# Routing sums its logits by matrix products and takes row numbers from the one-hot; one k load and one transposing transfer are ordered behind the first expert's weights

## The chip, the cores and the metric

The kernel runs on one core of a Trainium2 chip. Times are device microseconds of that core, from the start to the end of one launch. Engines are named as in the profile: PE multiplies matrices (PEld is its loading of the stationary operand), DVE, ACT and POOL do elementwise work, and SP issues most of the DMA transfers in this kernel (some are issued from ACT's queue). Each engine and each queue takes its instructions in a fixed order.

## The reference

Three layers follow one another. The first is attention with random features, for 4 batches of 8 heads, 576 rows and 64 columns: `phi(x) = exp(x·omega − |x|²/2 − max)`, then `kv = phi(k)ᵀ·v`, `num = phi(q)·kv`, divided by `phi(q)·Σphi(k)`. The second is a mixture of 8 experts over the 2304 resulting rows of 512 columns:

```python
logits = x @ w_gate
expert_idx = np.argmax(logits, axis=1)
probs = softmax(logits); gate_w = probs[row, expert_idx]
out[mask] = gate_w[mask, None] * (np.maximum(xe @ w1[e], 0.0) @ w2[e])
```

The third is a dense layer `(h * sigmoid(1.702 h)) @ w_out` with `h = x @ w_in` and 2048 columns in the middle.

## The kernel before

Attention is done in eight steps, two for each batch, of four heads each. `kgen(i)` does the k side of step i (projections "P" in `ph_P`, then `kv`), `qgen(i)` the q side (projections P, transposes X, the product N with `kv`, and the transposes R of the finished rows into `xh` and `xl`). Inputs are loaded by `load_qk` (L237). From the sixth operand on, `halves_T` (L286) splits an operand into two halves of 16 bits (ACT L297, POOL L298) and turns them by a transposing DMA issued on SP (L299); the turned tile `xT` has three buffers, so a transfer waits until the projections of three operands ago are through.

When a batch of 576 rows is done, `route_steps(b)` (L510) finds its expert. The logits come as two parts, from the high and the low half of `w_gate`, in one tile `lT` of 16 rows (8 experts by two parts) and 576 columns. Five PE transposes (L527) turn `lT`, DVE copies the result (L532, L533) and adds the two parts (L535). A row maximum (L539) and a comparison (L541) give the one-hot `oh`. A product with ones (L551) counts the rows of each expert, DVE finds the most frequent expert and writes its number `es` (L558 to L561), SP loads that number into a register (L594), and `pump` and `stage` (L669, L650) then issue the loads of this expert's weights (L664). For the rows that chose otherwise (`eq`, `rr`, a general path at the end), the number of each row's own expert is needed: five times a maximum of eight and an index search on DVE (L578, L579), and a copy (L581).

The expert's weights come in 8 parts (4 of `w1`, 4 of `w2`). For the first batch the first part is loaded in two pieces; the first seven parts have places of their own, so that eight transfers can be issued at once. Each part is split into high (ACT L686) and low (L688, on DVE for the first part and for the last batch's expert, else on POOL), and `moe_gen` multiplies (L128, tile `m_ps`, three products for each operand pair).

The program is written as generators: `attention_gen` merges `qgen(i)`, `kgen(i+1)` and a pending `route` by weight, and from the end of the first routing on a planner takes turns between attention and experts by the work done on each side. A scheduler then fixes the order on each engine by its own timeline; `tc.high_priority()` lifts the loads of the first expert's weights (L661). A manual dependency of the kind `NoSync` between two instructions only fixes their order in that schedule.

Of the kernel before, what the change touches and what calls it, by code (L numbers as in the profile page):

```python
# [8 lines left out]
F32 = mybir.dt.float32  # L9
# [13 lines left out]
def kernel(  # L23
# [91 lines left out]
    def behind(ins, n):  # L115
# [3 lines left out]
        for x in found:  # L119
# [3 lines left out]
                reason="behind",  # L123
            )

    def mm3(ps, ah, al, bh, bl, start, stop, pin=False):
# [45 lines left out]

    QH = 4
    NJ = 9
    NQ = B * (H // QH)
    clock = [0]
    late = []

# [55 lines left out]

    NB = QH * T + 2

    def load_qk(src, dst, i):  # L237
        b, qd = divmod(i, H // QH)
        h0 = qd * QH
        m = att.tile([P, NB, D], F32, tag="m", name="m", bufs=2)  # L240
        step = 2 if i < 1 else QH
        for h in range(0, QH, step):
            nc.sync.dma_start(
                out=m[:, h * T:(h + step) * T].rearrange("p (h t) d -> p h (t d)", h=step),
                in_=src[b, h0 + h:h0 + h + step, 0:T * P, :].rearrange("h (p t) d -> p h (t d)", t=T),
            )
        for pr in range(2):
            nc.sync.dma_start(
                out=m[pr * TAIL:(pr + 1) * TAIL, QH * T:],
                in_=src[b, h0 + 2 * pr:h0 + 2 * pr + 2, T * P:S, :].rearrange("h s d -> s h d"),  # L250
            )
        dst[i] = m

    sides = [0]
# [28 lines left out]
            square_sum(m, c, sq, FOLD)  # L283
        src[i] = (xT, sq, True)

    def halves_T(src, i, eng):  # L286
        sides[0] += 1
        if sides[0] <= FPX:
            return turned(src, i)
        if sides[0] - 1 in LO_DVE:  # L290
            eng = nc.vector
        m = src[i]
        hl = att.tile([P, NB, 2, D], F16, tag="hl", name="hl", bufs=2)
        xT = att.tile([P, NB, P], F16, tag="xT", name="xT", bufs=3)
        sq = att.tile([P, NB], F32, tag="sq", name="sq", bufs=3)
        for c in (slice(0, 8), slice(8, NB)) if i < FINE else (slice(0, NB),):
            nc.scalar.activation(out=hl[:, c, 0], in_=m[:, c], func=ACTF.Copy)  # L297
            eng.tensor_tensor(out=hl[:, c, 1], in0=m[:, c], in1=hl[:, c, 0], op=ALU.subtract)  # L298
            XQ.dma_start_transpose(out=xT[:, c], in_=hl[:, c].rearrange("p n a d -> p (n a d)"))  # L299
            square_sum(m, c, sq, FOLD_LATE)  # L300
        src[i] = (xT, sq, False)

# [101 lines left out]
    def qgen(i):  # L404
        b, qd = divmod(i, H // QH)
        qi = i
        if i + 1 < NQ:
            load_qk(q, q_in, i + 1)
            halves_T(q_in, i + 1, nc.vector if i + 1 < DVE_LO else nc.gpsimd)
# [60 lines left out]
        for n, op in enumerate(Q_ORDER.split()):  # L470
            g = int(op[1])
            if op == "R0" and qd == 0:
                while x_done[0] < b - 1:
                    yield None
                xh_t[b] = (moe if b % 2 else xep).tile([P, KD, S], F32R, tag="xh", name="xh", bufs=1)
                xl_t[b] = (moe if b % 2 else xep).tile([P, KD, S], F32R, tag="xl", name="xl", bufs=1)
            if op[0] == "P":
                c = ph_P(i, src, qp, "qp", 3, g)
            else:
                c = {"X": X, "N": N, "R": XT}[op[0]](g)  # L480
            if n == 0 and i + 1 < NQ:
                load_v(i + 1)
            if n == KPRE and i + 2 < NQ:
                load_qk(k, k_in, i + 2)
                halves_T(k_in, i + 2, nc.vector if i + 2 < DVE_LO else nc.gpsimd)
            yield c
        c0 = qd * QH * D
# [9 lines left out]


    gate_t, reg_t = {}, {}

    def route(b):
        g = route_steps(b)
# [7 lines left out]
    def route_steps(b):  # L510
# [10 lines left out]
            nc.scalar.activation(out=lT[:, c], in_=lT_ps, func=ACTF.Copy)  # L521
        yield 2.0
        yield 0
        lg_ps = pp.tile([P, T + 1, 2, E], F32, tag="n", name="lg_ps", bufs=1)
        for t in range(T + 1):
            n = P if t < T else TAIL
            nc.tensor.transpose(  # L527
                lg_ps[:n, t].rearrange("p a e -> p (a e)"), lT[:, t * P:t * P + n], ident[:2 * E, :2 * E]
            )
        lg2 = att.tile([P, T + 1, 2, E], F32, tag="lg2", name="lg2", bufs=1)  # L530
        nc.vector.memset(lg2[:, T], 0.0)
        nc.vector.tensor_copy(lg2[:, 0:T], lg_ps[:, 0:T])  # L532
        nc.vector.tensor_copy(lg2[:TAIL, T], lg_ps[:TAIL, T])  # L533
        lg = att.tile([P, T + 1, E], F32, tag="lg", name="lg", bufs=1)
        nc.vector.tensor_tensor(out=lg, in0=lg2[:, :, 0], in1=lg2[:, :, 1], op=ALU.add)  # L535


        rm = att.tile([P, T + 1, 1], F32, tag="rm", name="rm", bufs=2)
        nc.vector.tensor_reduce(out=rm, in_=lg, axis=AX.X, op=ALU.max)  # L539
# [35 lines left out]
        mx = att.tile([P, T + 1, 8], F32, tag="lmx", name="lmx", bufs=1)  # L575
        ix = att.tile([P, T + 1, 8], U32, tag="lix", name="lix", bufs=1)
# [73 lines left out]
    def stage(b, c):  # L650
        e = reg_t[b]
        if c < NW:
            st = landing(b, c, [P, KD, nfw * P])
            src = w1[bass.ds(e, 1), :, c * nfw * P:(c + 1) * nfw * P].rearrange("o (k p) f -> p (o k) f", p=P)
        else:
            c2 = c - NW
            st = landing(b, c, [P, nfw, DM])
            src = w2[bass.ds(e, 1), c2 * nfw * P:(c2 + 1) * nfw * P, :].rearrange(
                "o (k p) d -> p (o k) d", p=P
            )  # L660
        with tc.high_priority() if b in HP_STAGE else nullcontext():  # L661
# [326 lines left out]
    if True:  # L988
# [6 lines left out]
        halves_T(q_in, 0, nc.vector if DVE_LO else nc.gpsimd)  # L995
        load_qk(k, k_in, 1)
        setup_wg()
        halves_T(k_in, 1, nc.vector if DVE_LO else nc.gpsimd)
        A, Mg = attention_gen(), moe_all()
        done_a = done_m = 0.0  # L1000
# [532 lines left out]
```

## Time and profile before

| | before |
|---|---|
| median of 3 runs | 769.03 us (768.45 to 770.22) |
| the profiled execution's own time | 769.27 us |
| its span, first to last instruction | 767.3 us |
| PE busy | 740.3 us (96%) |
| PEld busy | 717.7 us (94%) |
| DVE, ACT, POOL busy | 529.7 (69%), 338.2 (44%), 131.9 us (17%) |
| share of PE in the chain that ended last | 84% |
| mean granted clock of PE | 0.989 of full speed |

How to read it: the time outside the span is 1.97 us in this execution. PE is at work nearly all the time, so what a change is worth shows in the few stretches where PE stands still or has the lower clock, and in the number and length of PE's own instructions.

### The profile page before, as it was taken

How to read it: one execution, taken by the hardware profiler on the slowest of the kernel's cores; microseconds unless marked ns; L12 is line 12 of the kernel's file. 1: busy time of each engine (PE TensorE's matmuls, PEld its weight loads, DVE VectorE, ACT ScalarE, POOL GpSimd, SP SyncE). 2: the span in 40 equal slices, each digit the busy share in tenths (PEclk: the TensorE clock that was granted, in tenths of full speed). 3: DMA queues.
4: the chain of work that ended last, by engine and by line, in shares of the span. 5: the costliest groups of instructions: out<-in, count | busy, mean ns of one | idle time of the engine just before them, and what ended most of it. 6: DMA issues, size and time to landing. Idle time of an engine off the chain costs nothing.

```text
span 767.3 us, 14364 instructions
## 1 busy us (share of the span) xinstructions
PE 740.3 (96%) x5559; PEld 717.7 (94%) x5559; DVE 529.7 (69%) x1188; ACT 338.2 (44%) x638; POOL 131.9 (17%) x78
## 2 busy tenths in 40 slices
PE   7998699999999999999999999999999999999997
PEld 6877599999999999998999999999999999999997
DVE  5877767485876686565879649981368777777774
ACT  5555354334621432233427464454576434443331
POOL 3564277608600441000000000000000000000000
PEclk9999789999999999999999999999999999999999
DMA  6447683447825454199245558972978544443311
GB/s 157 119 132 183 160 264 84 133 118 218 184 60 161 142 186 126 49 247 283 60 152 187 186 179 277 326 256 100 343 263 302 176 138 138 136 123 122 116 29 32
DMA packets 136716, 127.59 MB, mean 166 GB/s; under 512 B 58176, under 2 KB 120896, under 8 KB 135744
## 3 DMA queue, kind: packets, MB, share of 16 engines
q1 hardware_dynamic: 123936, 98.85, 43.8%
q10 hardware_dynamic: 12704, 27.73, 10.3%
q8 instruction: 46, 0.75, 0.4%
q14 instruction: 30, 0.25, 0.1%
HBM read 79.68 MB, written 40.40 MB: 156 GB/s over the span
## 4 chain that ended last, share of the span: by engine, by line
PE 84%; DVE 7%; DMA 5%; ACT 1%; issue 1%; POOL 0%; SPq 0%; ACTq 0%; POOLq 0%
PE m_ps L128 19%; PE qa L1237 13%; PE qa L1134 13%; PE qm L1237 7%; PE w_ps L128 4%; PE pb L1237 3%; PE qm L1134 3%; PE num L434 3%; PE qu L1134 3%; PE kv_ps L392 3%; DMA st<-in_moe_w_dram 2%; PE pr L334 2%; PE qn L1134 2%; PE tq L420 2%; PE qt L1134 2%
## 5 line engine op out<-in xcount | busy, mean ns | idle before, releaser
L1134 PE MATMUL qa<-y,wi 128*128 128x384 f32 x576 | 109.2, 337 | 0.4 <-DVE g L889 0.4
L1134 PEld LDWEIGHTS qa<-y,wi 128*128 128x128 f32 x576 | 101.4, 188 | 0.8 <-DVE g L889 0.8
L128 PE MATMUL m_ps<-xh,wh 128*128 128x288 f32 x256 | 80.3, 314 | 6.6 <-ACT wh L686 4.2
L128 PE MATMUL m_ps<-xh,wl 128*128 128x288 f32 x256 | 77.9, 304 | 0.0
L128 PE MATMUL m_ps<-xl,wh 128*128 128x288 f32 x256 | 77.2, 302 | 0.0
L688 POOL TENSOR_TENSOR wl<-st,wh 128x1024 fp32r<-128x1024 f32 x23 | 55.2, 2405 | 85.9 <-ACT wh L686 84.5
L349 DVE TENSOR_REDUCE small<-pr 128x4 f32<-128x512 f32 (+1 forms) x80 | 51.1, 638 | 9.6 <-PE pr L341 6.0
L128 PEld LDWEIGHTS m_ps<-xh,wh 128*128 128x128 f32 x256 | 49.5, 193 | 8.3 <-ACT wh L686 4.4
L686 ACT ACTIVATE wh<-st 128x1024 fp32r<-128x1024 f32 (+1 forms) x33 | 33.8, 1032 | 49.4 <-DMA st<-in_moe_w_dram 33.7
L723 DVE SCALAR_TENSOR_TENSOR h1l<-m_ps,h1h 128x288 fp32r<-128x288 f32 x64 | 28.8, 453 | 30.3 <-ACT h1h L720 30.3
L128 PEld LDWEIGHTS m_ps<-xl,wh 128*128 128x128 f32 x256 | 49.4, 193 | 0.2
L128 PEld LDWEIGHTS m_ps<-xh,wl 128*128 128x128 f32 x256 | 49.4, 193 | 0.2
L720 ACT ACTIVATE h1h<-m_ps 128x288 fp32r<-128x288 f32 x64 | 25.7, 407 | 51.8 <-PE m_ps L128 49.9
L128 PE MATMUL m_ps<-h1h,wh 128*128 128x288 f32 x160 | 48.3, 302 | 0.0
L128 PE MATMUL m_ps<-h1l,wh 128*128 128x288 f32 x160 | 48.1, 301 | 0.0
L128 PE MATMUL m_ps<-h1h,wl 128*128 128x288 f32 x160 | 47.8, 299 | 0.0
L1237 PE MATMUL qa<-p,p 128*128 128x256 f32 x360 | 46.1, 283 | 1.1 <-DVE p L843 0.8
L1237 PE MATMUL qa<-p,gs 128*128 128x256 f32 x360 | 45.9, 282 | 0.0
L1237 PEld LDWEIGHTS qa<-p,p 128*128 128x128 f32 x360 | 44.2, 190 | 1.6 <-DVE p L843 1.0
L1237 PEld LDWEIGHTS qa<-p,gs 128*128 128x128 f32 x360 | 44.2, 189 | 0.0
L434 PEld LDWEIGHTS num<-kv,qpT 128*128 128x128 f32 (+1 forms) x320 | 37.1, 186 | 5.4 <-ACT qpT L422 2.7
L434 PE MATMUL num<-kv,qpT 128*128 128x65 f32 (+1 forms) x320 | 39.5, 268 | 2.3 <-ACT qpT L422 1.4
(213 smaller groups left out, 1817.3 us busy)
## 6 DMA issues: line engine op xcount, KB each, us to landing
g_dram<-g ACTq DMA_DIRECT2D x48, 384.0 KB, 4.1
st<-in_moe_w_dram SPq DMA_DIRECT2D x31, 512.0 KB, 4.9
pg<-g_dram SPq DMA_DIRECT2D x10, 1024.0 KB, 5.5
raw<-in_moe_w_in_dram SPq DMA_DIRECT2D x16, 512.0 KB, 4.1
gt<-g_dram SPq DMA_DIRECT2D x8, 1024.0 KB, 5.5
p<-wo_dram SPq DMA_DIRECT2D x6, 1024.0 KB, 7.2
yt<-y_dram SPq DMA_DIRECT2D x12, 384.0 KB, 6.0
vm<-in_v_dram SPq DMA_DIRECT2D x32, 128.0 KB, 3.1
```

The lines of the kernel that those rows point to most:

```text
L128: ins = nc.tensor.matmul(out=ps, lhsT=a, rhs=b, start=start and n == 0, stop=stop and n == 2)
L334: nc.tensor.matmul(out=ps[:, :, h2], lhsT=xT[:, (2 * pr + h2) * 2 + t0 // 2], rhs=wbd)
L349: nc.vector.tensor_reduce(out=pm, in_=ps[:, :w], axis=AX.X, op=ALU.max, negate=on_act)
L392: nc.tensor.matmul(out=kv_ps[:, h, :], lhsT=kp[j // 2][:, j % 2, h2, :], rhs=vm[:, h, t, :], start=(t == 0), stop=False,)
L420: nc.tensor.transpose(tq[:, c, h2], qp[i][:, c, h2, :], ident)
L434: nc.tensor.matmul(out=ps[:n, c, h2, :], lhsT=lhsT, rhs=kv[:, h, :])
L686: nc.scalar.activation(out=hi[:, :, s], in_=st[:, :, s], func=ACTF.Copy)
L688: eng.tensor_tensor(out=lo[:, :, s], in0=st[:, :, s], in1=f32(hi)[:, :, s], op=ALU.subtract)
L720: nc.scalar.activation(out=hh[:, f], in_=ps, func=ACTF.Relu)
L723: nc.vector.scalar_tensor_tensor(out=hl[:, f], in0=ps, scalar=0.0, in1=f32(hh[:, f]), op0=ALU.max, op1=ALU.subtract)
L1134: ins = nc.tensor.matmul(out=ps, lhsT=w[:, a, ks], rhs=y[:, b, kk], start=start and kk + m == 0, stop=kk == 1 and m == 2, skip_group_check ...
L1237: ins = nc.tensor.matmul(out=ps, lhsT=x[:, f], rhs=w[i][:, f], start=start and f + m == 0, stop=f == NP - 1 and m == 2, skip_group_check=True,
```

## The change

Routing: the five PE transposes of `lT` become five matrix products of the same columns of `lT` with `fold`, a matrix of 16 by 8 made once as the sum of two blocks of the identity. A product thereby adds the two parts, and the DVE addition goes, with the buffer `lg2` and its memset. The row's own expert number is now taken from the one-hot: `oh` is multiplied by `left` (8 minus the expert's number, made once), reduced by a maximum, and turned back by `8 − x`; the five maxima, five index searches and the copy go. The order of the transfers: in `qgen(3)` the transposing transfer of q's operand 4 and the three loads of k's operand 5 are ordered behind the last of the first expert's eight weight transfers on SP.

```diff
+    def follow(ins, first):
+        if first is not None:
+            tc.add_manual_dep(ins.ins, first.ins.name, DependencyInfo(NoSync, DATA), reason="follow")
...
-            XQ.dma_start_transpose(out=xT[:, c], in_=hl[:, c].rearrange("p n a d -> p (n a d)"))
+            follow(XQ.dma_start_transpose(out=xT[:, c], in_=hl[:, c]...), after)
...
+                q_in, i + 1, nc.vector if i + 1 < DVE_LO else nc.gpsimd, asked[-1] if i == QB + 1 else None
...
-                load_qk(k, k_in, i + 2)
+                load_qk(k, k_in, i + 2, asked[-1] if i == QB + 1 else None)
...
+    lg = att.tile([P, T + 1, E], F32, name="lg")
+    def setup_route():
+        nc.gpsimd.memset(lg[:, T], 0.0)
+        nc.vector.tensor_tensor(out=fold, in0=ident[:2 * E, 0:E], in1=ident[:2 * E, E:2 * E], op=ALU.add)
+        nc.vector.tensor_scalar(out=left, in0=iota8, scalar1=-1.0, scalar2=float(E), op0=ALU.mult, op1=ALU.add)
...
-            nc.tensor.transpose(lg_ps[:n, t]..., lT[:, t * P:t * P + n], ident[:2 * E, :2 * E])
-        lg2 = att.tile([P, T + 1, 2, E], F32, tag="lg2", name="lg2", bufs=1)
-        nc.vector.memset(lg2[:, T], 0.0)
-        nc.vector.tensor_copy(lg2[:, 0:T], lg_ps[:, 0:T])
-        nc.vector.tensor_copy(lg2[:TAIL, T], lg_ps[:TAIL, T])
-        nc.vector.tensor_tensor(out=lg, in0=lg2[:, :, 0], in1=lg2[:, :, 1], op=ALU.add)
+            nc.tensor.matmul(out=lg_ps[:n, t], lhsT=lT[:, t * P:t * P + n], rhs=fold)
+        nc.vector.tensor_copy(lg[:, 0:T], lg_ps[:, 0:T])
+        nc.vector.tensor_copy(lg[:TAIL, T], lg_ps[:TAIL, T])
...
-        for t in range(T + 1):
-            nc.vector.max(mx[:, t], lg[:, t])
-            nc.vector.max_index(ix[:, t], mx[:, t], lg[:, t])
-        nc.vector.tensor_copy(ixf, ix[:, :, 0:1])
+        nc.vector.tensor_tensor(out=oh, in0=oh, in1=left.unsqueeze(1).to_broadcast([P, T + 1, E]), op=ALU.mult)
+        nc.vector.tensor_reduce(out=ixf, in_=oh, axis=AX.X, op=ALU.max)
+        nc.vector.tensor_scalar(out=ixf, in0=ixf, scalar1=-1.0, scalar2=float(E), op0=ALU.mult, op1=ALU.add)
...
-                nc.sync.dma_start(out=st[:, :, s], in_=src[:, :, s])
+                ins = nc.sync.dma_start(out=st[:, :, s], in_=src[:, :, s])
+                if b == 0 and c < 2 * NW - 1:
+                    asked.append(ins)
```

## Rows read from the trace of the kernel before

**Rows 1.** Busy time of engines by stretch: start:end, length, busy us (instructions), clock, DMA share, GB/s.
```profile
80.00:90.95 10.95, 8.86 (x72) 7.60 (x71) 10.30 (x61) 4.24 (x14) 1.17 (x1) 0.69 0.69 169
90.95:95.20 4.25, 0.00 (x1) 0.01 (x1) 0.02 (x1) 0.69 (x2) 0.00 (x0) 0.90 0.74 220
...
110.00:767.30 657.30, 647.26 (x4898) 636.08 (x4896) 452.89 (x921) 281.88 (x487) 80.48 (x37) 1.00 0.53 165
```
**Rows 2.** Chain of waits, 74 to 97 us: start, length, work.
```profile
76.75 0.38 PE lg_ps L527 x5
...
78.46 1.30 DVE lg L535
...
79.99 0.07 DVE lmx L578
...
82.95 0.07 DVE ixf L581
...
86.86 0.06 DVE es L561
...
88.41 6.08 DMA st<-in_moe_w_dram
...
94.51 0.64 ACT wh L686
```
**Rows 3.** Timeline of PE, 64 to 112 us: start, length, instruction, [idle before, releaser].
```profile
95.20 0.61 PE L128 MATMUL m_ps<-xh,wh 128*128 128x288 f32 x1 [4.25 <-ACT wh L686]
```
**Rows 4.** Timeline of SP's queue, 84 to 90 us: start, length, transfers issued.
```profile
85.04 1.81 SPq L299 DMA_TRANSPOSE xT<-hl  x1
86.95 0.53 SPq L243 DMA_DIRECT2D m<-in_k_dram  x1
88.41 1.55 SPq L664 DMA_DIRECT2D st<-in_moe_w_dram  x3
```
**Rows 5.** Lines L535 and L551 by themselves: ns min/median/max, first to last start.
```profile
L535 DVE TENSOR_TENSOR lg<-lg x4: 200/200/1348, 78.4 to 317.1; 128x40 f32<-128x40 f32 x4
...
L551 PEld LDWEIGHTS ct_ps<-oh,ones x8: 187/190/337, 83.5 to 321.1; 128*128 128x128 f32 x8
```
**Rows 6.** Timeline of POOL, 60 to 110 us.
```profile
77.60 2.11 POOL L257 TENSOR_TENSOR m<-m 128x1152 f32<-128x1152 f32 x1
79.78 1.39 POOL L262 TENSOR_TENSOR m<-m 128x576 f32<-128x576 f32 x1
```
**Rows 7.** DMA issues by line: count, KB each, median us to landing.
```profile
m<-in_k_dram SPq DMA_DIRECT2D x2, 256.0 KB, 2.9
...
st<-in_moe_w_dram SPq DMA_DIRECT2D x2, 256.0 KB, 6.2
```
**Rows 8.** Busy time by stretch, as in rows 1, for one microsecond.
```profile
91.00:92.00 1.00, 0.00 (x0) 0.00 (x0) 0.00 (x0) 0.00 (x0) 0.00 (x0) 1.00 0.36 103
```
**Rows 9.** Timeline of all engines around the last routing's weights, 324 to 336 us.
```profile
325.68 1.06 SPq L664 DMA_DIRECT2D st<-in_moe_w_dram  x2
...
330.30 1.06 ACT L686 ACTIVATE wh<-st 128x1024 fp32r<-128x1024 f32 x1 [1.99 <-DMA st<-in_moe_w_dram]
...
331.27 0.69 ACT L720 ACTIVATE h1h<-m_ps 128x288 fp32r<-128x288 f32 x2
...
331.71 0.66 PE L128 MATMUL w_ps<-h1h,wh 128*128 128x288 f32 x3 [0.62 <-ACT h1h L720]
...
333.04 0.40 PE L128 MATMUL m_ps<-xh,wh 128*128 128x288 f32 x1 [0.67 <-DVE h1l L723]
```
**Rows 10.** Busy time by stretch, as in rows 1, where PE's clock changed or held.
```profile
94.40:101.00 6.60, 5.80 (x25) 5.79 (x26) 3.16 (x8) 3.61 (x7) 2.38 (x1) 0.50 1.08 374
333.30:336.60 3.30, 3.30 (x16) 3.30 (x16) 1.28 (x2) 1.02 (x2) 0.00 (x0) 0.50 1.27 214
47.00:50.00 3.00, 1.48 (x10) 1.04 (x10) 2.73 (x8) 1.00 (x4) 2.84 (x3) 1.00 0.62 139
```
**Rows 11.** Groups of PE instructions by line, 87.2 to 128.5 us.
```profile
L340 PE MATMUL pr<-wh,xT 128*128 128x128 f16 x36 | 5.0, 224 | 0.0
```

More of the change, by code (lines that the diff above doesn't have):

```diff
@@ L124, in behind @@
             )
+    def follow(ins, first):
+        if first is not None:
+            tc.add_manual_dep(
+                ins.ins, first.ins.name,
+                mybir.DependencyInfo(mybir.DependencyClass.NoSync, mybir.DependencyReason.DATA),
+                reason="follow",
+            )
     def mm3(ps, ah, al, bh, bl, start, stop, pin=False):
@@ L174 @@
     NJ = 9
-    NQ = B * (H // QH)
+    QB = H // QH
+    NQ = B * QB
+    asked = []
     clock = [0]
@@ L235, with load_qk @@
     NB = QH * T + 2
-    def load_qk(src, dst, i):
+    def load_qk(src, dst, i, after=None):
         b, qd = divmod(i, H // QH)
@@ L242, in load_qk @@
         for h in range(0, QH, step):
-            nc.sync.dma_start(
+            follow(nc.sync.dma_start(
                 out=m[:, h * T:(h + step) * T].rearrange("p (h t) d -> p h (t d)", h=step),
                 in_=src[b, h0 + h:h0 + h + step, 0:T * P, :].rearrange("h (p t) d -> p h (t d)", t=T),
-            )
+            ), after)
         for pr in range(2):
-            nc.sync.dma_start(
+            follow(nc.sync.dma_start(
                 out=m[pr * TAIL:(pr + 1) * TAIL, QH * T:],
                 in_=src[b, h0 + 2 * pr:h0 + 2 * pr + 2, T * P:S, :].rearrange("h s d -> s h d"),
-            )
+            ), after)
         dst[i] = m
@@ L284, in turned, with halves_T @@
         src[i] = (xT, sq, True)
-    def halves_T(src, i, eng):
+    def halves_T(src, i, eng, after=None):
         sides[0] += 1
@@ L298, in halves_T @@
             eng.tensor_tensor(out=hl[:, c, 1], in0=m[:, c], in1=hl[:, c, 0], op=ALU.subtract)
-            XQ.dma_start_transpose(out=xT[:, c], in_=hl[:, c].rearrange("p n a d -> p (n a d)"))
+            follow(
+                XQ.dma_start_transpose(out=xT[:, c], in_=hl[:, c].rearrange("p n a d -> p (n a d)")), after
+            )
             square_sum(m, c, sq, FOLD_LATE)
@@ L408, in qgen @@
             load_qk(q, q_in, i + 1)
-            halves_T(q_in, i + 1, nc.vector if i + 1 < DVE_LO else nc.gpsimd)
+            halves_T(
+                q_in, i + 1, nc.vector if i + 1 < DVE_LO else nc.gpsimd, asked[-1] if i == QB + 1 else None
+            )
         src, kv = q_in.pop(i), kv_t.pop(i)
@@ L499 @@
     gate_t, reg_t = {}, {}
+    lg = att.tile([P, T + 1, E], F32, name="lg")
+    lgx = att.tile([P, 2, E], F32, name="lgx")
+    fold, left = lgx[:2 * E, 0], lgx[:, 1]
+    def setup_route():
+        nc.gpsimd.memset(lg[:, T], 0.0)
+        nc.vector.tensor_tensor(out=fold, in0=ident[:2 * E, 0:E], in1=ident[:2 * E, E:2 * E], op=ALU.add)
+        nc.vector.tensor_scalar(out=left, in0=iota8, scalar1=-1.0, scalar2=float(E), op0=ALU.mult, op1=ALU.add)
     def route(b):
@@ L523, in route_steps @@
         yield 0
-        lg_ps = pp.tile([P, T + 1, 2, E], F32, tag="n", name="lg_ps", bufs=1)
+        lg_ps = pp.tile([P, T + 1, E], F32, tag="n", name="lg_ps", bufs=1)
         for t in range(T + 1):
             n = P if t < T else TAIL
-            nc.tensor.transpose(
-                lg_ps[:n, t].rearrange("p a e -> p (a e)"), lT[:, t * P:t * P + n], ident[:2 * E, :2 * E]
-            )
-        lg2 = att.tile([P, T + 1, 2, E], F32, tag="lg2", name="lg2", bufs=1)
-        nc.vector.memset(lg2[:, T], 0.0)
-        nc.vector.tensor_copy(lg2[:, 0:T], lg_ps[:, 0:T])
-        nc.vector.tensor_copy(lg2[:TAIL, T], lg_ps[:TAIL, T])
-        lg = att.tile([P, T + 1, E], F32, tag="lg", name="lg", bufs=1)
-        nc.vector.tensor_tensor(out=lg, in0=lg2[:, :, 0], in1=lg2[:, :, 1], op=ALU.add)
+            nc.tensor.matmul(out=lg_ps[:n, t], lhsT=lT[:, t * P:t * P + n], rhs=fold)
+        nc.vector.tensor_copy(lg[:, 0:T], lg_ps[:, 0:T])
+        nc.vector.tensor_copy(lg[:TAIL, T], lg_ps[:TAIL, T])
         rm = att.tile([P, T + 1, 1], F32, tag="rm", name="rm", bufs=2)
@@ L574, in route_steps @@
         nc.vector.tensor_copy(cif, ci[:, 0:1])
-        mx = att.tile([P, T + 1, 8], F32, tag="lmx", name="lmx", bufs=1)
-        ix = att.tile([P, T + 1, 8], U32, tag="lix", name="lix", bufs=1)
-        for t in range(T + 1):
-            nc.vector.max(mx[:, t], lg[:, t])
-            nc.vector.max_index(ix[:, t], mx[:, t], lg[:, t])
         ixf = att.tile([P, T + 1, 1], F32, tag="ixf", name="ixf", bufs=1)
-        nc.vector.tensor_copy(ixf, ix[:, :, 0:1])
+        nc.vector.tensor_tensor(out=oh, in0=oh, in1=left.unsqueeze(1).to_broadcast([P, T + 1, E]), op=ALU.mult)
+        nc.vector.tensor_reduce(out=ixf, in_=oh, axis=AX.X, op=ALU.max)
+        nc.vector.tensor_scalar(out=ixf, in0=ixf, scalar1=-1.0, scalar2=float(E), op0=ALU.mult, op1=ALU.add)
         eq = att.tile([P, T + 1, 1], F32, tag="eq", name="eq", bufs=1)
@@ L997 @@
         setup_wg()
+        setup_route()
         halves_T(k_in, 1, nc.vector if DVE_LO else nc.gpsimd)
```

## The prediction

> **What bounds the kernel now.** I read the shares on the profile's first lines, then the engines by stretch, then what PE waited for, and last the chain of waits and SP's queue where PE stood still. The reader is to see that from 110 us to the end PE is busy for 647.26 of 657.30 us at full clock [rows 1]. After 110 us only a shorter or a smoother PE stream helps. The start is different: from 80 to 90.95 us PE is busy for 8.86 of 10.95 us at a mean clock of 0.69 while DVE is busy for 10.30 [rows 1], so DVE sets the pace there; then PE does nothing for 4.25 us until the first expert's weights are there and split by ACT [rows 1, 3]. That is the longest stop of PE. The chain says what leads to it: DVE's routing work up to the expert's number `es` at 86.92 us, the issue of the first weight transfer at 88.41, its landing 6.08 us later, 0.64 us of ACT, and PE at 95.20 [rows 2, 3]. Behind 95.20 PE has work all the time, so an earlier start there moves the end almost one for one. A small second place of the same kind stands at 330 us, below.
>
> **The change part by part.** All sums are against the profiled execution's own 769.27 us, which lies 0.24 us above the median of 769.03; I take 0.24 off at the end.
>
> *DVE ahead of `es`, first routing.* The chain has 1.30 us for the addition L535, and eight pieces of L578, L579 and L581 between 79.99 and 83.02 us that come to 1.23 us (the addition, the first and the last of the eight stand in [rows 2]). Both go: 2.53 us, the upper end. The three new instructions have the shapes of neighbours that cost about 0.1 us each in the chain, and by program order they stand behind `es`: 0 to 0.28 us. The lower end comes from the addition's 1.30 us being mostly a wait: in the three other routings the same instruction takes 0.20 us, here 1.35 [rows 5], and it ends at 79.76 us, when POOL's instruction of 77.60 to 79.71 us is over [rows 6]. Two more DVE instructions with both operands in the same memory follow (L541, L544), and POOL's next such instruction lasts until 81.17 us [rows 6]; if they stand still in its place, only 1.23 − 0.28 = 0.95 us remain. The Trainium skill has this as a rule: on its page "SBUF — State Buffer", section "SBUF: two separate sides", DVE and POOL share one port pair as an exclusive lock, which a DVE instruction with two operands in SBUF needs against a POOL instruction that reads SBUF, and the loser stands still for the whole instruction. The trace agrees (1.35 us against 0.20). By that rule the wait moves from the addition to the comparison rather than goes, and `es` gains the 0.95 us and not the 2.53. I take 1.5 us, nearer to the lower end, because POOL's second instruction is in the trace at the place where the comparison would come, and because PE at the lower clock limits the rest.
>
> *SP's queue.* Ahead of the weights SP issues the transposing transfer of q's operand 4 at 85.04 us (1.81 us, it waited for a buffer) and the first load of k's operand 5 at 86.95 (0.53 us) [rows 4]. `es` was ready at 86.92, so of the two only the k load delayed the register load, by 0.55 us. With `es` 1.5 us earlier, at 85.4, the transposing transfer would have stood in the way until 86.85; the order keeps that gain. First issue: 88.41 − 1.5 − 0.55 = 86.35 us. Behind the weights, SP must now issue the transposing transfer and three k loads, about 2 + 3 × 0.6 us, while it had little to do. Who waits for them: the turned tile of q's operand 4 is not read before 128.3 us, since the 36 pairs of projections from 87.2 to 128.5 us are just those of q's operand 3 and k's operand 4 [rows 11], 18 pairs each being the half of it; and k's operand 5 lacked its two small loads until after 104 us anyway. I cost the move at nothing; the cover is some 25 us for the one, some microseconds for the other.
>
> *The landing.* The first weight piece (256 KB) took 6.08 us. Loads of k of the same size took 2.9 us at the start of the kernel [rows 7]. The k load's 512 KB were in the queue just ahead, and the traffic falls to 103 GB/s when they are through [rows 8], so the weights are slow to start by themselves too. Ends: 0 and 3.2 us saved. I take 0.8 us, near the lower end, for the k load's share, since the low traffic with nothing else in the queue is the nearest row. So the first expert product starts at 95.20 − 1.5 − 0.55 − 0.8 = 92.35 us: **−2.85 us**.
>
> *The products on PE.* Five transposes took 0.38 us on the chain, 0.076 each [rows 2]. The count's product L551 of the same kind as the new ones appears as 8 records for 4 products [rows 5]: an f32 product is two records. Ten records at the transposes' 0.076 are 0.76 us: +0.38 per routing. Lower end 0 (one record as before), upper end ten records at a full weight load of 0.19 us [rows 5], +1.52. I take 0.4, because the weights are the same 16 rows. The first routing lies where DVE sets the pace; three others lie where PE is busy throughout: **+1.2 us** (0 to 4.6, or 6.1 with the first).
>
> *The last routing.* There the weights of the last expert are issued at 325.68 us and ACT waits 1.99 us for them, with an activation (h1h) queued behind that wait which PE needs: PE stops for 0.62 and for 0.67 us [rows 9], and its clock then is at half speed, 1.2 GHz, for 3.3 us [rows 10]. The index searches stand there in front of the memset of `oh`, so the count can come about 1 us sooner. The first stop goes with that and a part of the second: 0 to 1.29 us, I take **−0.9**. What is late next is the low part's split on DVE.
>
> In the second and third routing DVE's shorter work hides under PE. The setup instructions run in the first microseconds beside loads. Sum: 769.27 − 2.85 − 0.9 + 1.2 = 766.72; less 0.24: **766.5 us**.
>
> **The rivals.** (a) *The clock holds.* From 94.4 to 101 us PE has half clock, and its 25 records take 5.80 us [rows 10]; at full clock they would take 2.9. It held at full speed over 47 to 50 us, where PE was idle for 1.52 of 3 us [rows 10]. With a shorter stop (about 2.9 us instead of 4.25) it might hold: 766.5 − 2.9 = 763.6, and with the 3.3 us at 333 us spared too (−1.65) 762.0. Against it: at 333 us two stops of 1.29 us together were followed by the lower clock [rows 9, 10]. (b) *Only half arrives.* The comparison waits for POOL, the landing keeps its 6.08 us and the last routing stays as its schedule is: −0.95 − 0.55 + 1.2, some 768.7 us. (c) *The start does not move*, because PE's fixed order puts other waits ahead of it: the products alone remain, 770.2. (d) *Slower: the products are dear.* If each of the ten records costs a whole weight load of 0.19 us, the four routings cost 6.1 us against 3.75 gained: 771.4. It decides from about 0.16 us per record (3.75 us over three routings of ten records, and the 0.38 that go). For it: PEld is busy for 94% of the span, and the weight loads of L551 are that long. Against it: the transposes with the same 16 rows follow one another at 0.076.
>
> **How the numbers follow.** Forecast 0.44 (own range 765.0 to 768.0), clock holds 0.18, half 0.18, no move 0.06, dear products 0.14. About 0.2%, 1.5 us, is what a measurement of this kernel tells from no change: faster is below 767.5, slower above 770.6. Faster: 0.38 of the forecast, 0.18 of (a), 0.05 of (b), 0.61. Same: 0.05 of the forecast, 0.12 of (b), 0.05 of (c): 0.22. Slower: (d), and a little of the others by a changed schedule, 0.17. The range runs from 762.5 to 770.4: it leaves out most of (d) and the far end of (a).
>
> **What would show it.** In the changed kernel's trace: `es` near 85.4 us and the first weight issue near 86.4 with no k load and one transposing transfer less ahead of it; landing near 91.6; PE's stop near 3 us instead of 4.25, ending near 92.4. L541 or L544 at 1 us or more shows the wait for POOL moved. The products' records show as 20 or 40 in number, with 0.8 us or 1.9 per routing. PE's two stops before 333 us shrink to one. A stop of PE for the tile of q's operand 4 or k's operand 5 between 100 and 135 us would show the move of the transfers as wrong, and the prediction is wrong if the first expert product still starts after 94 us, or if new stops of PE behind 110 us exceed 2 us.

## The result, and the profile after

The changed kernel takes 775.38 us (median of 6 runs, 770.71 to 776.2) where the kernel before took 768.1 (6 runs): a ratio of 1.0084, 95% interval 1.0064 to 1.0105, so it is slower. The same kernel timed again with more runs gave 770.43 against 766.49, 1.0042 (1.0025 to 1.006). The two intervals do not overlap, and why is not settled; in both it is slower. Forecast were 766.5 us, a gain, with a range of 762.5 to 770.4 us; the second set's 770.43 lies at the upper end of that range, the first set's 775.38 far above it.

The profiled execution took 775.58 us, its span is 773.7 us (before: 767.3). First the engines by stretch, columns as in [rows 1]: around the first expert's weights, from there to the end, and two stretches at half clock.

```profile
80.00:94.65 14.65, 11.83 (x111) 10.15 (x110) 12.17 (x54) 6.49 (x20) 4.90 (x3) 0.88 0.37 73
94.65:95.50 0.85, 0.00 (x0) 0.00 (x1) 0.02 (x1) 0.68 (x2) 0.00 (x0) 1.00 1.12 319
110.00:773.70 663.70, 649.26 (x4898) 637.38 (x4896) 455.02 (x875) 280.13 (x484) 79.64 (x37) 0.99 0.54 167
48.00:55.00 7.00, 6.19 (x23) 5.11 (x24) 5.40 (x17) 2.68 (x6) 5.59 (x3) 0.52 0.13 29
178.00:183.00 5.00, 5.00 (x21) 4.66 (x22) 2.74 (x7) 2.60 (x4) 3.23 (x3) 0.50 0.57 160
```

The stop of 4.25 us is down to 0.85. But the first expert product stands at 95.50 us, not earlier than the 95.20 of [rows 3], the rest is 6.4 us longer than the 657.30 of [rows 1], and the clock is at half at 48 us and at 178 us, where before it was not. The chain of waits says how the work came to these places (start, length, what):

```profile
73.73 0.31 PE lT_ps L541
...
90.59 0.06 DVE es L576
...
91.37 3.42 DMA st<-in_moe_w_dram
94.82 0.64 ACT wh L700
...
156.73 1.19 PE lg_ps L549 x10
...
164.55 6.84 DMA m<-in_k_dram
...
172.57 0.40 ACT h1h L734
...
173.45 1.70 DVE eq L595
...
175.52 1.80 DVE rr L598
...
177.39 0.34 DVE xn L459
```

`es` comes at 90.59 us where it came at 86.86 [rows 2]. From the routing's first product on PE (73.73 us; 69.87 before) to `es` it takes 16.9 us, 17.0 before: the edits together brought 0.1 us there. Two terms of opposite sign stand behind that, as the timeline shows (PE's group, DVE's first copy of its result; first the kernel before, then the changed one):

```profile
76.68 0.45 PE L527 MATMUL lg_ps<-ident,lT 16*128 16x16 f32 x5
...
78.09 0.21 DVE L532 COPY lg<-lg_ps 128x64 f32<-128x64 f32 x1
```

```profile
80.55 1.26 PE L549 MATMUL lg_ps<-lgx,lT 16*128 16x8 f32 x10
...
83.09 0.18 DVE L550 COPY lg<-lg_ps 128x32 f32<-128x32 f32 x1
...
90.50 0.15 DVE L576 CAST es<-ci 128x1 int32<-128x1 uint32 x1
```

From the copy to `es` DVE takes 7.41 us where it took 8.68 (`es` starts at 86.77 us on the timeline before): 1.27 us less. But the copy comes 2.54 us after PE's group begins, 1.41 before: 1.13 us more, since the group is longer and more of attention's DVE work stands in front of the copy.

From `es` to the first expert product it takes 4.9 us instead of 8.3; how much of that is the orders' is seen in e9 to e11. The products take 1.19 us in the second routing, where the transposes took 0.38 at the same place. And there is a new chain at 164 to 178 us. The timeline shows its pieces (start, length, engine, line; in brackets how long the engine had stood and for whom):

```profile
83.65 1.41 POOL L272 TENSOR_TENSOR m<-m 128x576 f32<-128x576 f32 x1
...
83.81 1.31 DVE L556 TENSOR_TENSOR oh<-lg,rm 128x40 f32<-128x40 f32 x1
...
91.37 4.44 SPq L676 DMA_DIRECT2D st<-in_moe_w_dram  x8
...
95.50 0.40 PE L136 MATMUL m_ps<-xh,wh 128*128 128x288 f32 x1 [0.85 <-ACT wh L700]
...
171.50 1.17 ACT L307 ACTIVATE hl<-m 128x1152 f16<-128x1152 f32 x1 [4.50 <-DMA m<-in_k_dram]
...
172.57 0.39 ACT L734 ACTIVATE h1h<-m_ps 128x288 fp32r<-128x288 f32 x1
...
172.74 2.38 POOL L308 TENSOR_TENSOR hl<-m,hl 128x1152 f16<-128x1152 f32 x1 [22.00 <-ACT hl L307]
...
172.99 0.46 DVE L737 SCALAR_TENSOR_TENSOR h1l<-m_ps,h1h 128x288 fp32r<-128x288 f32 x1 [4.20 <-ACT h1h L734]
...
173.37 1.78 DVE L595 TENSOR_SCALAR eq<-ixf,cif 128x5 f32<-128x5 f32 x1
...
175.20 2.11 POOL L267 TENSOR_TENSOR m<-m 128x1152 f32<-128x1152 f32 x1
...
175.44 1.88 DVE L598 SCALAR_TENSOR_TENSOR rr<-eq,ixf 128x5 f32<-128x5 f32 x1
...
177.64 1.15 DVE L603 TENSOR_TENSOR total<-total,hit 128x1 f32<-128x1 f32 x1
...
177.86 1.94 PE L448 MATMUL num<-kv,qpT 128*128 128x65 f32 x8 [3.19 <-DVE xn L459]
```

In the first routing the comparison `oh` now ends with POOL's instruction, as the addition did before [rows 5, 6]. In the second, ACT stands 4.50 us in front of a load of k, and an h1h is queued behind it; DVE stands 4.20 us for that h1h with `eq`, `rr` and `total` queued behind its own h1l. When they are let go, POOL has begun, and three instructions of about 0.2, 0.17 and 0.14 us take 1.78, 1.88 and 1.15 us. PE waits 3.19 us and then works at half clock for 5 us.

**One account for all kernels.** Up to the start of the dense layer (before 401.65 us, after 407.12; from there all kernels take 365.4 to 367.5 us) I split the time into what PE stood still, what half clock took from it (busy time times one minus the granted clock, both summed over stretches of one microsecond), and the rest, PE's own work at full clock. Stops and half clock together, by stretch, in us:

| kernel, execution | 0–70 | 70–100 | 100–200 | 200–320 | 320–dense | sum | PE's own work |
|---|---|---|---|---|---|---|---|
| before | 8.7 | 13.4 | 0.6 | 0.3 | 4.4 | 27.4 | 374.2 |
| before, a second one (e9) | 8.3 | 9.7 | 0.3 | 0.3 | 3.5 | 22.1 | 374.5 |
| after | 11.7 | 8.5 | 7.2 | 0.4 | 2.1 | 29.9 | 377.2 |
| after, a second one (e5) | 11.0 | 9.8 | 3.7 | 0.3 | 2.2 | 27.0 | 376.4 |

Between the two profiled executions that are compared, the change is +2.5 us of stops and half clock, +3.0 of PE's own work and +0.9 behind, 6.4 us in all. The gains are there (70–100 us and the last routing), and so are three losses: PE's own work, 100–200 us, and 0–70 us. Between the two second executions (e9 and e5) it is +4.9, +1.9 and +1.2 us, and there 70–100 us gains nothing (9.7 and 9.8).

### The profile page after: what moved, and what is told of

The parts are those of the page before. It is cut to its first block, busy times and chain, and to the rows that moved or that the text cites. A ratio compares the mean times of both kernels' runs of the same rounds, so it can differ in the third digit from the quotient of the medians.

```text
span 773.7 us, 14346 instructions
## 1 busy us (share of the span) xinstructions
PE 743.8 (96%) x5579; PEld 719.9 (93%) x5579; DVE 531.3 (69%) x1130; ACT 337.8 (44%) x638; POOL 132.2 (17%) x79
## 4 chain that ended last, share of the span: by engine, by line
PE 82%; DVE 8%; DMA 5%; issue 2%; ACT 2%; SPq 1%; ACTq 0%; DVEq 0%
PE m_ps L136 17%; PE qa L1252 13%; PE qa L1149 13%; PE qm L1252 7%; PE num L448 4%; PE w_ps L136 3%; PE pb L1252 3%; PE qm L1149 3%; PE qu L1149 3%; PE kv_ps L404 3%; DMA st<-in_moe_w_dram 3%; DMA m<-in_k_dram 2%; PE pr L346 2%; PE tq L434 2%; PE qn L1149 2%
## 5 line engine op out<-in xcount | busy, mean ns | idle before, releaser
L136 PE MATMUL m_ps<-xh,wh 128*128 128x288 f32 x256 | 78.2, 306 | 2.0 <-DVE h1l L737 1.0
L136 PE MATMUL m_ps<-xh,wl 128*128 128x288 f32 x256 | 75.7, 296 | 0.2 <-DVE wl L702 0.2
L361 DVE TENSOR_REDUCE small<-pr 128x4 f32<-128x512 f32 (+1 forms) x80 | 51.1, 639 | 11.1 <-PE pr L353 7.2
```

The lines of the kernel that those rows point to most:

```text
L361: nc.vector.tensor_reduce(out=pm, in_=ps[:, :w], axis=AX.X, op=ALU.max, negate=on_act)
```

## The experiments

The expectations name their theories by letters, anew for each run. The theories after the result: **meetings** (a load, POOL and DVE meet at 170 us and PE loses a stop and its clock), **products** (ten records in each routing on a busy PE), **orders** (the orders themselves make the stops) and **redrawn** (any edit moves the planner's order, and with it stops come and go). e13 to e15 ran on another chip than e1 to e12; each time is set beside the kernel before on the same chip, so the ratios compare.

**e1, both orders alone**, on the kernel before.

```
-  halves_T(q_in, i + 1, ...)                 load_qk(k, k_in, i + 2)
+  halves_T(q_in, i + 1, ..., asked[-1] if i == QB + 1 else None)
+  load_qk(k, k_in, i + 2, asked[-1] if i == QB + 1 else None)
```

> The kernel before with the two orders behind the weights alone; routing is as before. Theory A (the orders give what they were meant to, and the loss is routing's): issue to first expert product shrinks from 8.3 us after the expert's number to about 5, so the first product starts near 92 us and the time is 763.5 to 765.5 us. Theory B (the order of the transfers itself brings the new stops, at 173 and 178 us, because the next loads of k and q come later and closer together): the stop of 3 us near 178 is there too and the time is 770 to 774. Theory C (any edit redraws the schedule, and stops come and go by chance): the stretch before 70 us differs from the kernel before although nothing in it was edited, and the time lies anywhere from 764 to 774.

Measured: 770.4 us, ratio 1.0064 (1.0038 to 1.009). PE, POOL and DVE on the timeline:

```profile
91.54 0.61 PE L136 MATMUL m_ps<-xh,wh 128*128 128x288 f32 x1 [0.56 <-ACT wh L701]
...
285.57 2.38 POOL L703 TENSOR_TENSOR wl<-st,wh 128x1024 fp32r<-128x1024 f32 x1 [0.72 <-ACT wh L701]
...
285.69 2.55 DVE L904 TENSOR_TENSOR z<-z 128x256 f32<-128x256 f32 x1
...
289.12 0.65 PE L448 MATMUL num<-kv,qpT 128*64 128x65 f32 x8 [1.73 <-DVE xn L459]
```

The first expert product comes at 91.54 us, 3.7 earlier than in [rows 3]; 1.1 us of that is an earlier begin of the routing (68.76 us against 69.87), and a second execution of the kernel before has it at 92.25 us (e9). PE's order is as before up to this product and another one from there on, and new stops came: here `z` stands behind POOL for 2.55 us (two more of it take 0.87 together right after). 70–100 us holds 11.1 us, 200–320 holds 4.0. From the first expert product to the dense layer it takes 309.4 us, before 306.5 and 304.4 (e9). The stop near 178 us that theory B asks for is absent (100–200 us: 0.1).

**e2, the routing edits alone**: from the changed kernel the orders taken out.

```
-  load_qk(k, k_in, i + 2, asked[-1] if i == QB + 1 else None)      (and in halves_T for q)
+  load_qk(k, k_in, i + 2)
```

> The changed kernel without the two orders: routing by products and row numbers from the one-hot. Theory A: products cost 0.8 us in each routing (1.19 against 0.38 us in the traces), so 2.4 to 3.2 us, and the expert's number gains next to nothing: 770 to 773 us. Theory B: the stops at 173 and 178 us are absent and the time is 768.5 to 771. Theory C: anywhere from 764 to 774, with a stop that no other kernel has.

Measured: 771.56 us, 1.0076 (1.0048 to 1.0104). The stop near 177 us is there too (2.70 us; `eq`, `rr` and `total` at 1.79, 1.88 and 1.15 us), so the orders do not make it. PE's own work is 375.4 us.

**e3, the products alone**, on the kernel before.

```
-  nc.tensor.transpose(lg_ps[:n, t]..., lT[:, t * P:t * P + n], ident[:2 * E, :2 * E])
-  nc.vector.tensor_tensor(out=lg, in0=lg2[:, :, 0], in1=lg2[:, :, 1], op=ALU.add)
+  nc.tensor.matmul(out=lg_ps[:n, t], lhsT=lT[:, t * P:t * P + n], rhs=fold)
```

> The kernel before with the products alone: 40 records of the new product line, 1.2 us per routing instead of 0.38. By its own cost 770.5 to 771.5 us. The addition of 1.3 us that waited for POOL in the first routing goes; if the wait is the port's and not the addition's, the comparison behind it takes about 1.3 us in its place. Theory C: stops elsewhere, 766 to 775.

Measured: 778.7 us, 1.0161 (1.0124 to 1.0198), above every range that was expected. PE's own work is 376.4 us; the rest of the loss are stops that neither kernel has (0.99, 0.72, 1.70 and 2.87 us between 261 and 302 us).

**e4, the row numbers from the one-hot alone**, on the kernel before.

```
-  for t in range(T + 1): nc.vector.max(mx[:, t], lg[:, t]); nc.vector.max_index(ix[:, t], ...)
+  tensor_tensor(oh * left); tensor_reduce(max); tensor_scalar(E - x)
```

> The kernel before with the row numbers from the one-hot alone: some 45 short DVE instructions fewer in all, no PE instruction more. By its own cost 767 to 768.1 us, the expert's number up to 1.2 us earlier in the first routing. If later DVE instructions of the routing (the comparison with the batch's expert and the one behind it) run into POOL's work as in the changed kernel (1.8 and 1.9 us instead of 0.2), a stop of PE of 1 to 3 us appears and the time is 770 to 772.

Measured: 766.88 us, 1.000 (0.9976 to 1.0023); PE's own work is 372.6 us. From the routing's first product on PE to `es` it takes 16.1 us, 16.9 before: without the products the searches' 0.8 us arrive in full.

**e5, the changed kernel again**, nothing altered.

> The changed kernel unaltered, run beside the others of this set: 775.4 us, ratio to before 1.0084. It tells which of its stops belong to the order of its instructions and which to one execution. Up to 70 us its instructions stand in the same order as before on every engine (but for three instructions of the setup), so I expect that the half clock at 49 to 53 us, which cost 3.0 us in the profile shown, is an execution's own: there in some profiles and not in others. The stop of 3.19 us at 178 us I expect again, between 2 and 4 us, since ACT's copy of the halves (L307) stands ahead of h1h (L734) in its order.

Measured: 770.43 us, 1.0042 (1.0025 to 1.006). `eq` and `rr` take 1.80 and 1.88 us again, the stop is 1.96 us this time, and the half clock at 48 us is there.

**e6, one instruction put back in its place**: ACT's copy for that load of k behind the h1h.

```
-  nc.scalar.activation(out=hl[:, c, 0], in_=m[:, c], func=ACTF.Copy)
+  follow(nc.scalar.activation(out=hl[:, c, 0], in_=m[:, c], func=ACTF.Copy), head)
   ...
+  heads.append(nc.scalar.activation(out=hh[:, f], in_=ps, func=ACTF.Relu))   # head is heads[-1] for i == 5
```

> The changed kernel with one instruction moved: ACT's copy of the halves of the k load that lands at 171 us (L307) is ordered behind the h1h (L734) that stood behind it. PE's order, DVE's and the products stay almost as they are. Theory A (the loss is a meeting: that h1h waits 4.5 us for a landing, eq, rr and total fall behind it into POOL's span and take 1.78, 1.88 and 1.15 us, PE stops 0.75 and 3.19 us and works at half clock for five more): 775.4 - 3.9 - 3.3 = 768.2, say 767 to 771, with eq and rr at 0.2 us and no stop over 1 us between 170 and 185. Theory B (the loss is the products' own time on TensorE, and the stop is made up elsewhere): no change, 774 to 777.

Measured: 769.17 us, 1.0019 (1.0 to 1.0039), beside 770.43 of e5 in the same set. The timeline and two stretches:

```profile
168.78 0.22 DVE L597 TENSOR_SCALAR eq<-ixf,cif 128x5 f32<-128x5 f32 x1
...
169.82 0.12 DVE L600 SCALAR_TENSOR_TENSOR rr<-eq,ixf 128x5 f32<-128x5 f32 x1
...
170.05 2.39 POOL L309 TENSOR_TENSOR hl<-m,hl 128x1152 f16<-128x1152 f32 x1 [19.79 <-DVE hit L604]
170.27 2.18 DVE L605 TENSOR_TENSOR total<-total,hit 128x1 f32<-128x1 f32 x1
...
177.41 1.06 ACT L702 ACTIVATE wh<-st 128x1024 fp32r<-128x1024 f32 x1 [6.33 <-DMA st<-in_moe_w_dram]
...
179.74 0.44 PE L469 MATMUL tx<-ident,xn 128*128 128x128 f32 x2 [1.19 <-DVE xl L478]
```

```profile
170.00:178.00 8.00, 8.00 (x66) 7.62 (x66) 3.68 (x7) 1.67 (x4) 4.50 (x2) 1.00 1.17 260
178.00:183.00 5.00, 3.81 (x22) 3.44 (x22) 1.86 (x6) 2.02 (x4) 4.45 (x3) 0.77 0.29 54
```

The meeting is as theory A has it: with `eq` and `rr` ahead of POOL they take 0.22 and 0.12 us, and PE is busy for all of 170 to 178 us. Its price is not. PE, further in its work now, runs into the next landing: ACT waits 6.33 us for the expert's weights, until 177.41 us, the activation `xh` stands behind that and DVE's `xl` behind `xh`, so PE stands still for 1.19 us up to 179.74, and half clock follows. Of 7.2 us (3.7 in e5) in 100–200 us 3.9 remain, and in the timed runs 1.3 us were won, which their scatter hardly tells from none.

**e7, the changed kernel without the products.**

```
-  nc.tensor.matmul(out=lg_ps[:n, t], lhsT=lT[:, t * P:t * P + n], rhs=fold)
+  nc.tensor.transpose(lg_ps[:n, t]..., ...)     # copies and addition as before
```

> The changed kernel without the products: the sums go back to transposes, a copy and an addition; both orders and the row numbers from the one-hot stay. Theory A (meetings): its order has eq, rr and total of the second routing in front of h1l, so no stop at 178; 766 to 770. Theory B (products cost 0.8 us in each of four routings): 775.4 - 3.2 = 772.2 if the other stops stay. Both: about 766, below before by up to 2 us. TensorE's time up to the dense layer less stops and half clock: 373.3 us as in the kernels without products, against 376.3 with them.

Measured: 780.7 us, 1.0172 (1.0144 to 1.0201): both theories missed it. PE's own work is 372.6 us, 4 us less than with products, as expected; but stops and half clock sum to 43.4 us, 20.4 of them after 200 us. One of them on the timeline, and the clock behind it:

```profile
298.40 1.06 ACT L703 ACTIVATE wh<-st 128x1024 fp32r<-128x1024 f32 x1 [6.18 <-DMA st<-in_moe_w_dram]
...
299.36 0.39 ACT L737 ACTIVATE h1h<-m_ps 128x288 fp32r<-128x288 f32 x1
...
299.81 1.09 PE L136 MATMUL w_ps<-h1h,wh 128*128 128x288 f32 x3 [2.20 <-ACT h1h L737]
```

```profile
300.00:306.00 6.00, 6.00 (x26) 5.55 (x27) 2.29 (x7) 2.20 (x5) 4.21 (x2) 0.50 0.37 127
```

It is the same pattern as at 171 us: an ACT instruction that waits for a landing stands in front of an h1h that PE needs.

**e8, every product twice** into the same place.

```
   nc.tensor.matmul(out=lg_ps[:n, t], lhsT=lT[:, t * P:t * P + n], rhs=fold)
+  nc.tensor.matmul(out=lg_ps[:n, t], lhsT=lT[:, t * P:t * P + n], rhs=fold)
```

> The changed kernel with every product issued twice into the same place: 10 more records of TensorE in each routing, 40 in all. Theory B (0.12 us for each record on the path): +4.8 us in TensorE's time up to the dense layer less stops and half clock, 381 us against 376 to 377; the whole time by itself 780, if the planner leaves the rest as it is, which it does not quite. If the products are hidden or cost what a plain transposition costs (0.04 us a record, 0.38 us for ten): +1.6 us.

Measured: 787.61 us, 1.0244 (1.0201 to 1.0288). PE's own work is 380.5 us, 3.3 to 4.1 over the changed kernel's: 0.08 to 0.10 us for each of the 40 more records. That is below theory B's 0.12. The expectation's lower price, 0.04, is half of what it should be: 0.38 us was for five transposes, 0.076 each, so 40 records at that price are 3.0 us and not 1.6. The run thus puts a record between 0.076 and 0.12 us and does not decide between them. The rest of the loss is again stops (38.1 us in sum). By line (ns lowest, median, highest; weight loads and products):

```profile
L549 PEld LDWEIGHTS lg_ps<-lgx,lT x40: 127/187/187, 80.0 to 326.5; 16*128 16x128 f32 x32, 16*64 16x64 f32 x8
L549 PE MATMUL lg_ps<-lgx,lT x40: 197/251/272, 80.0 to 326.5; 16*128 16x8 f32 x32, 16*64 16x8 f32 x8
L550 PEld LDWEIGHTS lg_ps<-lgx,lT x40: 133/187/187, 80.2 to 326.6; 16*128 16x128 f32 x32, 16*64 16x64 f32 x8
```

**e9, the kernel before again.**

> The kernel before unaltered, for a second profile of it: 766.5 us. In all five profiles of kernels with a routing edit and products or the one-hot taken on the second day of runs the clock was at half somewhere in 47 to 54 us, 1.7 to 3.3 us of TensorE's time, and in the one profile of before it was not. Up to 70 us the order of instructions is the same. Theory C (it belongs to the execution): half clock there in this profile too, about 3 us. Theory D (the edits bring it): none, as in the first profile.

Measured: 766.95 us, 0.9999 (0.9974 to 1.0023); the profiled execution took 764.12. No half clock at 48 us, and at the place on which the prediction was built:

```profile
91.30 0.63 ACT L686 ACTIVATE wh<-st 128x512 fp32r<-128x512 f32 x1 [1.51 <-DMA st<-in_moe_w_dram]
...
92.25 0.59 PE L128 MATMUL m_ps<-xh,wh 128*128 128x288 f32 x1
```

```profile
85.00:92.00 7.00, 6.48 (x42) 5.72 (x42) 4.93 (x23) 3.69 (x13) 0.00 (x0) 0.50 0.88 221
```

There is no stop in front of the first expert product. The weights landed 3.67 us after their issue and not 6.1, and PE was at half clock from 85 us on and busy when they came. Half clock took about as much from 70 to 100 us as in the first execution (4.9 and 5.1 us); what differs is the time in which PE stood still (4.8 and 8.3). The stop of 4.25 us was that one execution's.

**e10 and e11, each order alone** on the kernel before: e10 has the last line of e1's diff, e11 the one above it.

> The kernel before with one of the two orders: the k load behind the first expert's weights, the next q's transposing transfer where it was. If the k load is what the weights' first piece shares its transfer with, the piece lands about 3.4 us after its issue (6.08 before) and the first expert product stands at 92 to 92.5; if the transposing transfer in front keeps the queue, the first issue stays at 1.5 us after es and the product at 94 to 95. Time: that gain is mostly not kept in either case, 765.5 to 768.

> The kernel before with the other of the two orders: the transposing transfer behind the weights, the k load where it was. The first piece still lands in about 6 us, beside the k load: product at 94.5 to 95.5. Its order of instructions is redrawn more than the other's, so I expect a meeting somewhere after 100 us: 766 to 770, not faster than before.

Measured: the k load 766.73 us, 1.0001 (0.9979 to 1.0023); the transposing transfer 770.3, 1.0048 (1.0024 to 1.0073). From `es` to the first issue it takes 0.97 us with the k load behind the weights and 1.65 with only the transfer behind them (1.64 before, from the same timelines); from the issue to ACT's start 4.36 and 4.97 us. So the k load was what held SP, by 0.7 us. Neither order alone brings the landing of 3.4 us that was expected of the k load's. The transfer's order pays with stops at 200 to 320 us (3.8 us there).

**e12, the changed kernel with MAX and the index search**: e4's diff turned round.

> The changed kernel with the row numbers back from MAX and its index search; products and both orders stay. Its order of instructions on TensorE is nearly that of the changed kernel (42 of 3,400 lines differ). Whatever the one-hot saves is its difference to the changed kernel: es comes 1 to 1.5 us later in the first routing if DVE's 10 operations stood on the path, none later if the comparison's wait for POOL had taken their place. Time 770 to 773; the stop near 178 us stays, 2 to 3 us. TensorE's time up to the dense layer less stops and half clock 376 us, as with products.

Measured: 774.08 us, 1.0091 (1.006 to 1.0122). PE's own work is 377.1 us. `es` does not come later: from the copy to `es` it takes 7.31 us, with the one-hot 7.41, so beside the products the one-hot saves nothing there. Behind 320 us it has 6.0 us of stops and half clock where the changed kernel has 2.1 and 2.2. The other kernels bear that out in part: without products, e4, e14 and e15, which have the one-hot, hold 2.5 to 2.7 us there and the six executions that have not 3.3 to 4.6; but e7 and e8 hold 7.9 and 8.2 with it, e3 1.9 without it.

**e13, the three instructions of the setup alone**, their results unused; on each engine all others stand in the order of before.

```
+  nc.gpsimd.memset(lg0[:, T], 0.0)
+  nc.vector.tensor_tensor(out=fold, in0=ident[:2 * E, 0:E], in1=ident[:2 * E, E:2 * E], op=ALU.add)
+  nc.vector.tensor_scalar(out=left, in0=iota8, scalar1=-1.0, scalar2=float(E), ...)
```

> The kernel before with the three new instructions of the setup and nothing that uses them: a fill on POOL, a scaling and an addition on DVE, each about 0.1 us, in the first microseconds. Every other instruction stands where it stood. Theory D (the setup instructions bring the half clock at 48 to 54 us by moving the first landings and engines against each other): half clock there, 3 us of TensorE's time, and the time 1.5 to 3 us over before. Theory C (it belongs to the execution, or to something else): no difference in time, 0 plus or minus 1 us.

Measured: 769.54 us, 1.0033 (1.0005 to 1.006). The half clock is not at 48 but at 70 us, after a stop of 1.75 us in front of `small` L470 (the chain of waits leads back from it to a landing of k at 68.75 us), and the first expert product comes at 98.05 us:

```profile
70.44 0.36 PE L470 MATMUL small<-ident,xn 64*128 64x64 f32 x1 [1.75 <-DVE xl L477]
...
98.05 0.61 PE L136 MATMUL m_ps<-xh,wh 128*128 128x288 f32 x1 [2.52 <-ACT wh L709]
```

```profile
70.00:77.00 7.00, 6.46 (x29) 3.76 (x29) 5.77 (x15) 1.86 (x7) 5.88 (x3) 0.51 0.56 144
```

So three instructions of 0.1 us each cost something, by the interval 0.4 to 4.6 us, whose lower end is close to nothing; neither theory named the place, and by what path they do it stays open.

**e14, the one-hot with its setup instruction in the first routing**, on e4.

```
+  if b == 0:
+      nc.vector.tensor_scalar(out=left, in0=iota8, scalar1=-1.0, scalar2=float(E), ...)   # no longer in the setup
```

> The row numbers alone on the kernel before, as in the earlier run with a ratio of 1.000, with the one setup instruction (the falling numbers) moved from the start into the first routing. Theory D: no half clock at 48 to 54 us and 3 us less than that run, 763 to 765 (ratio 0.996). Theory C: the same as that run, ratio 1.000, 766 to 768.

Measured: 766.2 us, 1.000 (0.9976 to 1.0024), as e4. But the edit did not move the instruction: it waits for nothing of the routing, and the scheduler put it back into the first microseconds.

```profile
1.38 0.30 DVE L582 TENSOR_SCALAR lgx<-iota 128x8 f32<-128x8 f32 x1
```

In e4 it starts at 1.35 us, and the order of all engines up to the dense layer is e4's but for this instruction and the fill next to it. So this is e4 a second time, on another chip, and does not tell theories C and D apart. What it shows is the scatter of the clock: half clock at 48 to 54 us in e4, none there and half clock from 69 to 72 us here. Counted over all profiles, half clock falls between 47 and 77 us in 11 of 12 with a setup instruction (not in e2) and in one of five without (e10): theory D is neither shown nor refuted.

**e15, the k load's order and the one-hot**: e14 with the last line of e1's diff.

> The candidate for the best: row numbers from the one-hot and the k load behind the weights on the kernel before, without products and without the transposing transfer's order. TensorE's own time stays at 373 to 374 us up to the dense layer. If the last routing's gain stays (2.5 us of stop and half clock after 320 us where the changed kernel had 2.1 and before 3.5 to 4.4) and no new meeting is drawn: 763 to 766. If a meeting of the size seen in the others (2 to 6 us) is drawn: 768 to 771.

Measured: 768.16 us, 1.0027 (0.9999 to 1.0055). Stops came at 175 us and after 200 us (0.9 and 1.9 us). The setup instruction stands at 1.38 us here too. No kernel tried is faster than before.

## Why the prediction was wrong, step by step

**"Behind 95.20 PE has work all the time, so an earlier start there moves the end almost one for one."** This is the step that failed most. In e1 the start did move, by 3.7 us against the first execution and 0.7 against e9, and the end did not. In the changed kernel it takes 311.6 us (309.1 in e5) from the first expert product to the dense layer, where before it took 306.5 (304.4 in e9): some 5 us more behind the start, where the sum had 1.2 more and 0.9 less. Two things were missed. The stop of 4.25 us is one execution's: in e9 the weights land 2.4 us sooner after their issue, PE arrives when they do, and stops and half clock at 70–100 us are then 9.7 us and not 13.4. Against that, the changed kernel's 8.5 and 9.8 are a gain of 0 to 5 us, about 2.4 between the means. And work that follows is not in the order that it had: the planner and the scheduler put it together anew, so stops of 1 to 3 us, with half clock behind, come where there were none. That was a half sentence within the 0.17 for slower, though it is the largest term in e3, e7 and e8.

**`es` earlier by 1.5 us.** Measured 0.1, as the sum of a gain of 1.27 us and a loss of 1.13. The gain is near to the 1.5. The addition's wait went to the comparison (1.31 us, ending with POOL's instruction), as rival (b) had it. The Trainium skill's page "SBUF — State Buffer", section "SBUF: two separate sides", has the rule for this, and the trace agrees with it at this place (1.31 us against 0.33 for the same comparison before). The searches by themselves are worth 0.8 us (e4, e7), near to rival (b)'s 0.95. The loss is the term that failed: the products were left out of the first routing, "where DVE sets the pace", but with them DVE's copy comes 1.13 us later after PE's group begins. It is the same in every kernel with products (2.54 or 2.55 us; 1.18 to 1.41 in all without). That `es` came later by 3.7 us in the first profile is from the time before the routing; e5 has it at 89.4 us and e9 at 86.2.

**SP's queue 0.55 us, the landing 0.8.** The first was right: `es` to issue takes 0.78 us, 1.55 before, and e10 puts it on the k load. The second is about right in size and not certain: 3.42 us against 6.08 looks like 2.7 us, but from the issue to ACT's start the seven executions with both orders took 3.1 to 4.6 us (3.7 in the mean) and the seven with neither 3.7 to 6.1 (4.7). The difference of the means is 1.0 us, and the two ranges overlap.

**The products, +1.2 us.** Mis-sized: the chain has 1.19 us for ten records where the transposes took 0.38, so 0.8 in each of four routings, 3.2 us; PE's own work says the same (375.4 to 377.2 us in the six kernels' executions with single products, 372.5 to 374.5 in the ten without), and doubling them adds 3.3 to 4.1 more. The price lies between the two that I weighed, at 0.08 (e8) to 0.12 us a record; I had taken the transposes' 0.076 for a record whose weight load has a median of 187 ns; the transposes' has 136. The count of ten records was right. Rival (d) was the right direction with the wrong amount, and below its 0.16 it should not have decided; it did together with the rest. The first routing, which I left out, pays as well. (The eight pieces counted for the searches are seven in the view; their sum is right.)

**The last routing, −0.9 us.** Right in direction, and small: stops and half clock behind 320 us fell from 4.4 and 3.5 us to 2.1 and 2.2. The clock that stood at 0.50 at 333 us [rows 10] no longer falls, but in e9 it does not fall either. e12, without the one-hot, has 6.0; e7 and e8, whose orders are others, have more with it (7.9 and 8.2). So a gain of about 1 us is likely and not shown.

**"In the second and third routing DVE's shorter work hides under PE."** Failed in the second. Not the shorter work was the matter but what stands next to it: `eq`, `rr` and `total` behind an h1l that waits. Its cost in the profile is 7.2 us, 3.7 in e5; taken away (e6), it gives 1.3 us back in the timed runs, which is hardly told from none: PE then meets the next landing.

The two signs that the prediction named against itself, a first expert product after 94 us and new stops of more than 2 us behind 110 us, are both in the trace (95.50 and 3.19 us; 94.25 and 1.96 in e5).

What remains open: why the changed kernel's two sets of runs differ by 5 us, and whether and how the instructions of the setup cost some 3 us ahead of 70 us.

## What to carry to other kernels

A stop that one profile shows is a sample: look at a second execution before it is sold (4.25 us in front of the first expert product in one, none in the other). Price an f32 product from a row of an f32 product: ten records took 1.19 us here, where ten at the transposes' 0.076 are 0.76 and ten at a whole weight load of 0.19 are 1.9. Look in the trace whether an instruction that you moved did move (e14). And where a planner sets the order, an edit's largest effect can be the new neighbours of distant instructions; look there for what waits for a landing in front of something that PE needs, and for small DVE instructions that fall into POOL's span.

## What the hardware showed that I had not expected

DVE stands still for POOL also in very small instructions, and in one with a scalar for each partition: `eq` (128x5) 1.78 us against 0.22, `rr` 1.88 against 0.12, `total` (128x1) 1.15 and 2.18 against 0.14. Each of them ends with POOL's instruction. `xn`, one of whose operands is in PSUM, takes its usual 0.40 us at 177.31 us, while POOL works from 177.38.

The clock does not follow from the last stop alone: after a stop of 1.39 us at 48 us it fell to half in e5 and did not in e9, with the same order of work on PE ahead of it.
